# Linear attention and a squared-ReLU feed-forward on one core: the second batch's k^T v and x made two pairs at a time, both plans drawn anew

## The chip, the core and the metric

The kernel runs on one core of one Trainium2 chip. The metric is the device time of one execution in microseconds (us). A core has a matrix engine (TensorE, PE in the profile, with its weight loads as PEld), a vector engine (DVE), a scalar engine (ACT), a general engine (POOL) and a queue engine that issues most transfers (SP). PE writes to PSUM, in banks of 128 partitions x 512 floats; the other operands lie in SBUF.

## What is computed

```python
q_s = softmax(q, axis=-1)            # q, k, v: 8 batches, 8 heads, 576 tokens, 64 wide
k_s = softmax(k, axis=2)             # over the tokens
kv  = einsum('bhsd,bhse->bhde', k_s, v)
x   = einsum('bhsd,bhde->bhse', q_s, kv)   # laid out as 4608 tokens x 512
h   = maximum(x @ w_in, 0)           # 512 -> 2048
out = (h * h) @ w_out                # 2048 -> 512, float32
```

The weights come as 64-bit floats and are taken apart into a high and a low part of the PE's short format; x and h*h are split alike, so that a product takes three passes (high high, high low, low high).

## The kernel before

**Tiles of tokens and batches.** Each batch has 512 tokens ahead and a tail of 64. Tile t of the feed-forward takes the 512 tokens of batch t; the eight tails together make one more tile. While tile t runs, the attention of batch t + 1 is made between its products, in 16 steps of which four belong to each of the four pairs of heads: step s = 4p + i is part i of pair p. Tiles 0 and 1 are made straightforwardly: for each of 16 blocks f of the hidden width 12 products `h` (`first`), and two blocks later 12 products into the four banks `acc` (`second`). From tile 2 on a scheme with fewer products is used.

**Tile 0 also converts the weights.** For each of 16 units u, ACT scales the words (`scale_words`), DVE joins them by way of a PSUM bank named `up` (`join_words`: TENSOR_SCALAR into the bank, SCALAR_TENSOR_TENSOR out of it), POOL adds the low word, ACT casts the high part, and POOL subtracts to get the low part (`split_words`). The tiles `w` of it have two buffers.

**Attention before the change.** Batch 0 (start of the kernel) and batch 1 (beside tile 0) go pair by pair: `kv_of(b, p)` makes k^T v of a pair in one burst of products, scales it into the tile `kv`; `q_turn` transposes q with PE into the bank `qT` and copies it to SBUF, with POOL copying the 64 tail tokens (`qT<-qth`); `x_product(b, p, x)` makes x in two halves of 288 columns, each two products that use two of the four 64 x 64 quarters of the array, and copies each half out. From batch 2 on (`b >= TB`, TB = 2) two pairs go together: `kv_of(b, p-1, p)` in one burst into two banks, then `x_products`: four products of 512 columns, one in each quarter of the array, into the same two banks. The odd pair has its heads crossed over (`turn`), and the x of the tail tokens (`tail_burst`, eight products of 64 columns) is hung behind the next k^T v burst.

**Banks.** Up to the start of the feed-forward the intermediate results find six PSUM banks; after it just two, `a0` and `a1` (`bank`). In batch 1 these two serve the `up` of the conversion, the transposes (`qT`, `kmT`), the maximum's broadcast (`kmb`), k^T v and x.

**The order of the instructions** is made by `Planner`: it knows each step's engine, estimated length, and what it must wait for, and takes at each moment the most urgent of the steps that could start (`order`). The urgency is the estimated length of what depends on a step, altered by a list of random shifts (`shift`), each drawn from a seed: `SEEDS` for the first plan (the start and tile 0, `run`), `LATER` for the second (the rest up to tile 6, `run_on`). `possible` keeps a step from taking the last bank where its users could then not run; some of its clauses hold in the second plan alone (`self.locked`). The engines run their instructions in the order written.

**Names that the prediction uses.** In the profile `acc<-w,gh` and `acc<-w,gl` are `second`, `h<-x,w` is `first`, `kv<-v,ek` and `kv<-v_tail,kt` are k^T v; in batch 1 `x<-qT,kv` is x, from batch 2 on `kv<-qT,kv` is x (it is written into the banks of kv) and `kv<-qtail,kv` the tails. A 32-bit float product is two records. Line L101 is the helper that issues every planned instruction, so operands tell the steps apart.

Of the kernel before, what the change touches and what calls it, by code (L numbers as in the profile page):

```python
# [10 lines left out]
F32 = mybir.dt.float32  # L11
# [121 lines left out]
class Planner:  # L133
# [127 lines left out]
    def possible(self, n, b, known, spare):  # L261
        if n.end is not None:
            return True
        if n not in known:
            known[n] = all(
                o is b or o.placed is not None
                or self.locked and o.choices and o.users[0] is b.users[0]
                or (spare if len(o.choices) > 1 else self.place(o)[0] is not None)
                or self.locked and not o.choices and all(
                    self.possible(u, b, known, spare)  # L270
                    for u in (o.before.users if o.before else []) + (o.last.users[:1] if o.last else [])
                )
                for o in n.buffers
            ) and all(self.possible(o, b, known, spare) for o in n.before)
        return known[n]
# [106 lines left out]
def attention_ffn(  # L382
# [43 lines left out]
    STEP = 0.0  # L426
    WIDE = 487
    SEEDS = (
# [8 lines left out]
    )  # L437
    LATER = (
# [8 lines left out]
    )  # L447
    EASE = 0.0
    EARLY = 2
# [185 lines left out]
    def load_kq(b, p, which, queue=Y):  # L635
        turned = which == "k" and b == 0
        t = pair_tile(b, p, [P, C, 2, D] if turned else [P, 2, C, D], which)
        src = (k if which == "k" else q)[b, 2 * p:2 * p + 2, 0:M, :]
        to = "p c h d" if turned else "p h c d"
        queue.dma_start(out=t, in_=src.rearrange(f"h (p c) d -> {to}", c=C), kb=256)  # L640
        made[which, b, p] = t

# [40 lines left out]
    def load_tail_kq(b, which, queue=Y):  # L683

        src = k if which == "k" else q
        t = att.tile(
            [P, GH, D], F32, tag=f"{which}t", name=f"{which}t_{b}", bufs=1
        )
        for g in range(2):
            queue.dma_start(  # L690
                out=t[g * TL:(g + 1) * TL].only(2 * g, 2 * g + 1),
                in_=src[b, g * GH:(g + 1) * GH, M:SQ, :].rearrange("h p d -> p h d"),
                kb=64,
            )
        made[f"{which}t", b] = t
# [201 lines left out]
    def first_max(p):  # L897

        kr = made["k", 0, p].rearrange("p c h d -> p c (h d)")
        ps = bank(f"kT_{p}", True)  # L900
        with plan.together():
            for c in range(C):
                T.transpose(out=ps[:, c * P:(c + 1) * P], in_=kr[:, c, :], identity=ident, n=300)
        kc = small([P, 1], "kc", f"kc_0_{p}")
        V.tensor_reduce(out=kc, in_=ps, op=ALU.max, axis=AX.X)
        at = p % 2 * 2 + p // 2
        V.scalar_tensor_tensor(
            out=kc, in0=kc, scalar=-1.0, in1=made["ktm"][:, at:at + 1], op0=ALU.mult, op1=ALU.min, n=8
        )
        made["kT", p] = ps, kc  # L910

# [60 lines left out]
    def q_turn(b, p):  # L972

        qr = made.pop(("qn", b, p))
        ps = bank(f"qT_{b}_{p}", b == 0)
        with plan.together():
            for c in range(C):
                T.transpose(
                    out=ps[:, c * P:(c + 1) * P], in_=qr[:, c, :], identity=ident, n=260
                )  # L980
        qt = (boot if b == 0 and p % 2 else att).tile(
            [P, SQ], F32, tag="qh", name=f"qT_{b}_{p}", bufs=1
        )
        at = (p % 2 * 2 + p // 2) * TL
        G.tensor_copy(out=qt[:, M:SQ].only("tail"), in_=made["qTt", b][:, at:at + TL], n=64)
        V.tensor_copy(out=qt[:, 0:M].only("main"), in_=ps)
        made["qT", b, p] = qt

    def kv_product(b, *pairs):

        two = [bank(f"kv_{b}_{p}", b == 0) for p in pairs]
        made["kvp", b] = two
        n = D if b == 0 else D + 1
        tails = made.pop("tails", None) if b >= TB else None
        with plan.together():
            for p, ps in zip(pairs, two):
                kr, vr = made.pop(("ek", b, p)), made.pop(("v", b, p))
                tl, th = tail_of(b, p)
                turn = p % 2 if b >= TB else 0
                parts = [(kr[:, c, :], c) for c in range(C)]  # L1000
                if b == 0:
                    parts.append((made.pop(("ekt", p)), C))
                else:
                    parts.append((
                        made["kt", b][:, th, :].rearrange("p h d -> p (h d)").only(p % 2, p % 2 + 2), C
                    ))
                for k_part, c in parts:
                    for j in range(2):
                        rows = slice((j ^ turn) * D, (j ^ turn) * D + D)
                        cols = slice(j * (D + 1), j * (D + 1) + n)  # L1010
                        if b == 0:
                            of = vr[:, j, c, :] if c < C else v_heads[tl, 2 * p + j, 0:D].only(p // 2)
                        else:
                            of = vr[:, c, cols] if c < C else v_tail[:, p * W + cols.start:p * W + cols.stop]
                        T.matmul(
                            out=ps[rows, 0:n], lhsT=k_part[:, j * D:(j + 1) * D], rhs=of,
                            start=(c == 0), stop=(c == C),
                            n=2 * n if b < TB else 108 + BURST * (c == j == 0 and p == pairs[0]),
                        )
            if tails:  # L1020
                tail_burst(two, TAIL_AT, *tails)
        if tails:
            tail_out(two, TAIL_AT, *tails)
# [11 lines left out]
    def kv_of(b, *pairs):  # L1035

        kv_product(b, *pairs)
        kv_scale(b, *pairs)
        for p, ps in zip(pairs, made["kvp", b]):
            kv = small([P, D], "dg" if b >= TB and p > 1 else "kvs", f"kv_{b}_{p}")  # L1040
            S.activation(out=kv, in_=ps[:, 0:D], func=AF.Copy, scale=made.pop(("ks", p)), n=100)
            made["kv", b, p] = kv

# [139 lines left out]
    def first(t, f, x):  # L1183
# [8 lines left out]
        S.activation(out=r, in_=ps, func=AF.Relu)  # L1192
        if 0 < t < STRASSEN[0] and f >= ON_ACT:
            return r, r
        V.scalar_tensor_tensor(
            out=ps, in0=ps, scalar=0.0, in1=r, op0=ALU.max, op1=ALU.mult
        )
        return ps, r

    def split_g(t, f, ps, r):  # L1200
# [289 lines left out]
    def step_between(b, s, x):  # L1490

        p, i = divmod(s, NP)
        if b >= TB and i == 3 and p % 2:
            x_products(b, p, x, 0)

    def step_after(b, s, x, alone=True):
# [22 lines left out]
        elif i == 2:  # L1519
# [3 lines left out]
            else:  # L1523
                if p == 0:
                    tail_turn(b)
                kv_of(b, p)
                q_turn(b, p)
            if p + 1 < NP:
                load_v(b, p + 1)
# [2 lines left out]
                load_tail(b + 1)  # L1532
                load_tail_v(b + 1)
        elif i == 3:
            if b < TB:
                x_product(b, p, x)
            elif p % 2:
                x_products(b, p, x, 1)
            if p + 1 < NP:
                prepare(b, p + 1, alone)  # L1540
# [796 lines left out]
```

## Time and profile before

| | us |
|---|---|
| time, median of 3 runs (803.92 to 805.36) | 804.3 |
| time of the profiled execution | 804.34 |
| its span in the profile | 802.6 |
| PE busy | 786.7 (98%) |
| DVE busy | 597.3 (74%) |
| ACT busy | 497.3 (62%) |
| POOL busy | 139.1 (17%) |

The busy share of an engine is an average over stages with different limits: POOL's 17% over the span is nine tenths and more in the first sixth of it and next to nothing after. PE's products are pipelined and their ends modelled, so its cost is best read from one start to the next. The mean granted clock of the profiled run is 0.998 of full speed.

### The profile page before, as it was taken

How to read it: one execution, taken by the hardware profiler on the slowest of the kernel's cores; microseconds unless marked ns; L12 is line 12 of the kernel's file. 1: busy time of each engine (PE TensorE's matmuls, PEld its weight loads, DVE VectorE, ACT ScalarE, POOL GpSimd, SP SyncE). 2: the span in 40 equal slices, each digit the busy share in tenths (PEclk: the TensorE clock that was granted, in tenths of full speed). 3: DMA queues.
4: the chain of work that ended last, by engine and by line, in shares of the span. 5: the costliest groups of instructions: out<-in, count | busy, mean ns of one | idle time of the engine just before them, and what ended most of it. 6: DMA issues, size and time to landing. Idle time of an engine off the chain costs nothing.

```text
span 802.6 us, 14938 instructions
## 1 busy us (share of the span) xinstructions
PE 786.7 (98%) x5189; PEld 689.8 (86%) x5189; DVE 597.3 (74%) x1252; ACT 497.3 (62%) x967; POOL 139.1 (17%) x165
## 2 busy tenths in 40 slices
PE   8899999999999999999999999999999999999997
PEld 7578878888888989899898989898989888888887
DVE  6898985878768787787877777778776663246995
ACT  5898855545565667566756666666665665566452
POOL 4899892000000000000000000000000000000014
PEclk9999999999999999999999999999999999999999
DMA  9994116954699899898898978999898469999565
GB/s 288 390 327 143 31 49 176 328 150 124 177 265 253 265 275 279 238 272 247 263 266 271 263 216 258 240 283 259 259 280 257 138 218 368 381 306 377 169 181 98
DMA packets 210890, 193.19 MB, mean 241 GB/s; under 512 B 127424, under 2 KB 172992, under 8 KB 210816
## 3 DMA queue, kind: packets, MB, share of 16 engines
q1 hardware_dynamic: 205824, 189.96, 77.8%
q10 hardware_dynamic: 4352, 1.51, 0.8%
q0 software_dynamic: 640, 0.79, 0.4%
q8 instruction: 41, 0.67, 0.3%
q14 instruction: 33, 0.27, 0.1%
HBM read 150.34 MB, written 41.29 MB: 239 GB/s over the span
## 4 chain that ended last, share of the span: by engine, by line
PE 87%; DMA 6%; DVE 2%; ACT 2%; SPq 1%; issue 1%; POOL 1%; POOLq 0%; DVEq 0%; ACTq 0%
PE acc L101 34%; PE h L101 31%; PE h L1354 9%; PE out L2087 7%; PE kv L101 4%; DMA k<-in_k_dram 2%; SPq L101 1%; DMA raw<-in_moe_w_out_dram 1%; DMA raw<-in_moe_w_in_dram 1%; DMA ring<-w_sums 1%; PE x L101 1%; ACT w L101 1%; DMA out_dram<-o 1%; DVE w L101 1%; DMA bst<-bst 1%
## 5 line engine op out<-in xcount | busy, mean ns | idle before, releaser
L101 PE MATMUL acc<-w,gh 128*128 128x512 f32 x888 | 267.0, 382 | 3.7 <-DVE g L101 1.8
L101 PEld LDWEIGHTS acc<-w,gh 128*128 128x128 f32 x888 | 154.1, 190 | 24.3 <-issue 4.8
L101 PE MATMUL acc<-w,gl 128*128 128x512 f32 x444 | 168.4, 379 | 0.1
L101 PEld LDWEIGHTS h<-w,ring 128*128 128x128 f32 x1200 | 152.7, 191 | 11.8 <-issue 2.4
L101 PE MATMUL h<-w,ring 128*128 128x256 f32 x1200 | 155.2, 276 | 0.6 <-DVE c L101 0.5
L101 DVE TENSOR_TENSOR c<-h,u 128x256 f32<-128x256 f32 (+1 forms) x144 | 66.8, 466 | 86.3 <-ACT u L101 48.2
L101 ACT ACTIVATE c<-c 128x256 f32<-128x256 f32 (+1 forms) x198 | 116.3, 587 | 23.3 <-DVE c L101 20.1
L101 ACT COPY u<-h 128x256 f32<-128x256 f32 (+1 forms) x144 | 58.5, 406 | 95.2 <-PE h L101 76.5
L101 POOL PARTITION_ALL_REDUCE kmx<-km x24 | 20.6, 859 | 455.6 <-DVE km L101 392.6
L101 PEld LDWEIGHTS acc<-w,gl 128*128 128x128 f32 x444 | 83.9, 189 | 12.6 <-DVE gl L101 0.7
L101 PE MATMUL h<-x,w 128*128 128x512 f32 x384 | 90.6, 383 | 1.1 <-DVE x L101 0.6
L101 PEld LDWEIGHTS h<-x,w 128*128 128x128 f32 x384 | 71.3, 189 | 13.9 <-issue 1.7
L2087 PE MATMUL out<-w,w 128*128 128x512 f32 (+1 forms) x370 | 72.7, 352 | 0.6 <-DVE w L101 0.6
L2087 PEld LDWEIGHTS out<-w,w 128*128 128x128 f32 x370 | 62.7, 190 | 8.2 <-DVE w L101 0.8
L101 DVE TENSOR_TENSOR gl<-c,gh 128x512 fp32r<-128x512 f32 x80 | 54.9, 687 | 13.5 <-ACT gh L101 12.6
L101 PEld LDWEIGHTS h<-w,w 128*128 128x128 f32 x480 | 59.9, 191 | 3.9 <-issue 0.8
L101 PE MATMUL h<-w,w 128*128 128x256 f32 x480 | 61.8, 277 | 0.1
L101 ACT CAST gh<-c 128x512 fp32r<-128x512 f32 x80 | 49.5, 619 | 2.1
L1354 PE MATMUL h<-w,ring 128*128 128x512 f32 x204 | 46.3, 379 | 0.0
L101 DVE TENSOR_REDUCE bst<-q 128x18 f32<-128x576 f32 x48 | 35.9, 748 | 13.8 <-DMA q<-in_q_dram 10.3
L1354 PEld LDWEIGHTS h<-w,ring 128*128 128x128 f32 x204 | 38.6, 189 | 5.5
L101 POOL TENSOR_TENSOR w<-w,w 128x512 fp32r<-128x512 f32 x32 | 41.1, 1295 | 4.3 <-ACT w L101 4.1
(183 smaller groups left out, 1085.3 us busy)
## 6 DMA issues: line engine op xcount, KB each, us to landing
ring<-w_sums SPq DMA_DIRECT2D x48, 768.0 KB, 6.0
w<-w_sums SPq DMA_DIRECT2D x48, 512.0 KB, 5.3
ring<-w_sums SPq DMA_DIRECT2D x90, 256.0 KB, 4.7
k<-in_k_dram SPq DMA_DIRECT2D x32, 256.0 KB, 4.7
raw<-in_moe_w_in_dram SPq DMA_DIRECT2D x16, 512.0 KB, 8.4
raw<-in_moe_w_out_dram SPq DMA_DIRECT2D x16, 512.0 KB, 9.4
w<-wo_sums SPq DMA_DIRECT2D x32, 256.0 KB, 3.9
g_b<-c SPq DMA_DIRECT2D x30, 256.0 KB, 5.6
```

The lines of the kernel that those rows point to most:

```text
L101: getattr(self.eng, op)(*map(real, args), **{k: real(a) for k, a in kwargs.items()})
L1354: nc.tensor.matmul(out=out.real(), lhsT=a[:, k * P:(k + 1) * P].real(), rhs=in_turn(m[k]).real(), start=(begin and k == 0 and i == 0), sto ...
L2087: nc.tensor.matmul(out=banks[name][m][:, at].real(), lhsT=a[:, m * P:(m + 1) * P].real(), rhs=(rhs if half is None else rhs[:, half]).real ...
```

## The change

Batch 1 is made as the batches from 2 on are: pairs 0 and 1, and pairs 2 and 3, have their k^T v in one burst, with the odd pair's heads crossed over, and their x in four quarters of the array, 512 columns at once. The x of the tail tokens of pairs 0 and 1 hangs behind the k^T v burst of pairs 2 and 3, that of pairs 2 and 3 behind the first k^T v burst of batch 2, which runs beside tile 1. For this, q of an odd pair is loaded in two transfers with the heads exchanged (one before), q's tails in six (two before); POOL's copy of the tail tokens per pair goes, as x of the tails reads the transposed tail tile directly; odd pairs of batch 1 get a buffer `ql` of their own. In the planner the clauses of `possible` that were for the second plan hold in the first too. Both lists of seeds are replaced (63 by 57, and 58 by 48). In batch 0 one instruction of DVE that joins two maxima (`kc`) has another form with the same result. A branch for the squares of tile 0 is added that is never taken.

```diff
@@ Planner.possible
-                or self.locked and o.choices and o.users[0] is b.users[0]
+                or o.choices and o.users[0] is b.users[0]
...
-                or self.locked and not o.choices and all(
+                or not o.choices and all(
@@ SEEDS, LATER: all values replaced
@@ load_kq
+        if which == "q" and b and p % 2:
+            for h in range(2):
+                queue.dma_start(
+                    out=t[:, h].only(h), in_=src[1 - h].rearrange("(p c) d -> p c d", c=C), kb=128
+                )
@@ load_tail_kq
+        if which == "q" and b:
+            for g, (at, of) in itertools.product(range(2), ((0, 0), (2, 3), (3, 2))):
+                n = 1 + (at == 0)
+                queue.dma_start(
+                    out=t[g * TL:(g + 1) * TL, at:at + n, :].only((g, at)),
+                    in_=src[b, g * GH + of:g * GH + of + n, M:SQ, :].rearrange("h p d -> p h d"),
+                    kb=16 * n,
+                )
@@ first_max
-        V.scalar_tensor_tensor(
-            out=kc, in0=kc, scalar=-1.0, in1=made["ktm"][:, at:at + 1], op0=ALU.mult, op1=ALU.min, n=8
+        V.tensor_scalar(
+            out=kc, in0=kc, scalar1=-1.0, scalar2=made["ktm"][:, at:at + 1], op0=ALU.mult,
+            op1=ALU.min, n=8,
@@ q_turn
-            [P, SQ], F32, tag="qh", name=f"qT_{b}_{p}", bufs=1
+            [P, SQ], F32, tag="ql" if b and p % 2 else "qh", name=f"qT_{b}_{p}", bufs=1
...
-        at = (p % 2 * 2 + p // 2) * TL
-        G.tensor_copy(out=qt[:, M:SQ].only("tail"), in_=made["qTt", b][:, at:at + TL], n=64)
+        if b == 0:
+            at = (p % 2 * 2 + p // 2) * TL
+            G.tensor_copy(out=qt[:, M:SQ].only("tail"), in_=made["qTt", b][:, at:at + TL], n=64)
+        elif p % 2 == 0:
+            four = made["qTt", b].rearrange("p (i g t) -> p i g t", i=2, g=2)
+            made["qtail", b, p // 2] = four[:, :, p // 2, :]
@@ kv_product
-        tails = made.pop("tails", None) if b >= TB else None
+        tails = made.pop("tails", None)
...
-                turn = p % 2 if b >= TB else 0
+                turn = p % 2 if b else 0
@@ step_between
-        if b >= TB and i == 3 and p % 2:
+        if i == 3 and p % 2:
             x_products(b, p, x, 0)
@@ step_after
-                kv_of(b, p)
+                if p % 2:
+                    kv_of(b, p - 1, p)
                 q_turn(b, p)
...
-            if b < TB:
-                x_product(b, p, x)
-            elif p % 2:
+            if p % 2:
                 x_products(b, p, x, 1)
```

## Rows read from the trace of the kernel before

**Rows 1.** The page: busy time of each engine, and POOL's share by slice.

```profile
PE 786.7 (98%) x5189; PEld 689.8 (86%) x5189; DVE 597.3 (74%) x1252; ACT 497.3 (62%) x967; POOL 139.1 (17%) x165
...
POOL 4899892000000000000000000000000000000014
```

**Rows 2.** Windows: length, busy of PE, PEld, DVE, ACT, POOL, then clock, DMA, GB/s.

```profile
36.00:56.00 20.00, 17.08 (x80) 13.72 (x77) 18.86 (x30) 17.85 (x25) 19.17 (x18) 1.00 1.01 332
...
96.00:116.00 20.00, 20.00 (x116) 17.06 (x116) 18.42 (x33) 13.48 (x21) 18.49 (x17) 1.00 0.15 41
116.00:132.40 16.40, 16.40 (x97) 12.41 (x96) 10.74 (x23) 7.66 (x16) 7.74 (x9) 1.00 0.49 138
```

**Rows 3.** PE's waits over the span: total us, times, longest.

```profile
PE acc L101 <- DVE g L101: 1.8, 1, 1.8
...
PE acc L101 <- ACT o L101: 1.5, 1, 1.5
```

**Rows 4.** Chain of waits through batch 1: start, length, piece, count of records.

```profile
64.60 2.59 PE h L101 x12
...
70.43 0.63 PE x L101 x4
71.06 2.14 PE h L101 x9
...
90.30 0.73 PE kv L101 x20
91.03 2.79 PE acc L101 x12
93.82 1.12 PE x L101 x8
94.94 2.16 PE h L101 x9
```

**Rows 5.** The same chain through batch 2, made two pairs at a time.

```profile
173.37 1.32 PE kv L101 x40
174.68 0.84 PE acc L101 x3
...
178.76 1.02 PE kv L101 x8
179.78 2.14 PE acc L101 x9
...
198.76 1.59 PE kv L101 x48
200.35 1.49 PE h L101 x6
```

**Rows 6.** POOL and PE in order of time, and POOL's tail copies (56 to 132 us).

```profile
124.70 2.50 POOL L101 TENSOR_TENSOR w<-w,w 128x512 fp32r<-128x512 f32 x2 [2.25 <-ACT w L101]
...
128.53 0.59 PE L101 MATMUL acc<-w,gh 128*128 128x512 f32 x2
...
L101 POOL COPY qT<-qth 128x64 f32<-128x64 f32 x4 | 0.9, 234 | 0.1
```

**Rows 7.** DVE's instructions on `up` in a window; batch 2's copies of x.

```profile
56.00:120.00 64.00, 25.84 (x40) 1.00 0.30 95
...
180.02 0.68 DVE L101 COPY x<-kv 128x512 f32<-128x512 f32 x1
...
212.02 0.69 DVE L101 COPY x<-kv 128x512 f32<-128x512 f32 x1 [0.34 <-PE kv L101]
```

**Rows 8.** The start: DVE's kc, POOL beside it, and SP's loads of q's tails.

```profile
8.32 0.16 DVE L101 SCALAR_TENSOR_TENSOR kc<-kc,ktm 128x1 f32<-128x1 f32 x1
...
20.02 0.68 DVE L101 SCALAR_TENSOR_TENSOR kc<-kc,ktm 128x1 f32<-128x1 f32 x1
...
19.39 1.29 POOL L101 TENSOR_TENSOR w<-w,raw 128x512 int32<-128x512 int32 x1
...
L101 SPq DMA_DIRECT2D qt<-in_q_dram x2: 614/616/617, 18.6 to 19.3; - x2
```

More of the change, by code (lines that the diff above doesn't have):

```diff
@@ L639, in load_kq @@
         to = "p c h d" if turned else "p h c d"
+        if which == "q" and b and p % 2:
[3 more added lines that the diff above has]
+                )
+            made[which, b, p] = t
+            return
         queue.dma_start(out=t, in_=src.rearrange(f"h (p c) d -> {to}", c=C), kb=256)
@@ L688, in load_tail_kq @@
         )
+        if which == "q" and b:
[6 more added lines that the diff above has]
+                )
+            made[f"{which}t", b] = t
+            return
         for g in range(2):
@@ L1017, in kv_product @@
                             start=(c == 0), stop=(c == C),
-                            n=2 * n if b < TB else 108 + BURST * (c == j == 0 and p == pairs[0]),
+                            n=2 * n if b == 0 else 108 + BURST * (c == j == 0 and p == pairs[0]),
                         )
@@ L1039, in kv_of @@
         for p, ps in zip(pairs, made["kvp", b]):
-            kv = small([P, D], "dg" if b >= TB and p > 1 else "kvs", f"kv_{b}_{p}")
+            kv = small([P, D], "kvs" if b < TB or p < 2 else "dg", f"kv_{b}_{p}")
             S.activation(out=kv, in_=ps[:, 0:D], func=AF.Copy, scale=made.pop(("ks", p)), n=100)
@@ L1194, in first @@
             return r, r
-        V.scalar_tensor_tensor(
-            out=ps, in0=ps, scalar=0.0, in1=r, op0=ALU.max, op1=ALU.mult
-        )
+        if t == 0 and (False):
+            S.activation(out=ps, in_=r, func=AF.Square)
+        else:
+            V.scalar_tensor_tensor(
+                out=ps, in0=ps, scalar=0.0, in1=r, op0=ALU.max, op1=ALU.mult
+            )
         return ps, r
```

30 rows, old and new, of tables (LATER, SEEDS) are left out of this document.

## The prediction

> **What bounds the kernel now.** First the page: PE is busy 98% of the span, so time can be won where PE has less to do or stops waiting; POOL is busy in the first sixth alone [rows 1]. Then the windows of that sixth, for an average hides it: between 36 and 56 us PE lacks 2.9 us, and from there to the end of tile 0 it is busy without a gap (the two windows that are not shown are as full) [rows 2]. But up to 116 us DVE has 18.4 and 18.9 of 20 us and POOL 18.5 and 19.2: tile 0 is bounded by PE with two engines close behind it. Third, PE's waits: the two large ones are 1.8 us for a step of DVE at 48.8 us, before the stretch in question, and 1.5 us for a copy of ACT at 230 us [rows 3]. Last, the chain of waits: from 56 us until past the first pairs of batch 2 it holds PE and nothing else, product after product, with the bursts of batch 1 among them [rows 4] and those of batch 2, which are already made as the change makes batch 1's [rows 5]. So the change can be priced with rows of its own kind.
>
> **PE's bursts, step by step.** Twelve products of `h` take 2.59 us, 0.216 each [rows 4]. A burst costs its piece of the chain and what the piece behind it takes above 0.216 a product, which is the cost of changing over and back.
> - k^T v of one pair: 0.73 + (2.79 - 12 x 0.216) = 0.93. There are four such bursts, all of 0.73: 3.7 us.
> - x, a half alone: 0.63 + (2.14 - 9 x 0.216) = 0.83; four of them, 3.3 us. Two halves back to back: 1.12 + (2.16 - 9 x 0.216) = 1.34; two of these, 2.7 us.
> - Together 9.7 us; two of the ten are followed by a transpose and change over only once, about 0.05 less each: 9.6 us.
>
> After the change, by batch 2's rows [rows 5]:
> - k^T v of two pairs without tails: 1.32 + (0.84 - 3 x 0.216) = 1.51.
> - The same with eight products for tails behind it: 1.59 + (1.49 - 6 x 0.216) = 1.78, so tails cost 0.27.
> - x of two pairs: 1.02 + (2.14 - 9 x 0.216) = 1.22, twice: 2.44.
> - Together 1.51 + 1.78 + 2.44 = 5.73 us in tile 0, and 0.27 in tile 1, where batch 2's first burst now carries batch 1's last tails.
>
> So PE has 9.6 - 5.7 = 3.9 us less in tile 0 and 0.3 more in tile 1: **3.6 us less**. Most of it is x: 576 columns in two quarters become 512 in four, and six change-overs become two. None of this lay beside other PE work; all of it stands on the chain.
>
> **What else moves in tile 0.** The engines close behind PE decide how much comes through. POOL's last conversion ends at 124.70 + 2.50 = 127.20; the product that first reads it is the second of the three that begin at 128.53, so at 128.75 [rows 6]. The margin is 1.5 us. POOL loses four tail copies, 0.9 us [rows 6]. If POOL's order had no other play, tile 0 could end 1.5 + 0.9 = 2.4 us earlier, not 3.9. But POOL also waits 2.25 us just before that last conversion, for a cast of ACT, which in the window is busy 7.7 of 16.4 us [rows 2, 6]; the new order may close part of that. I take the middle of 2.4 and 3.9, 3.15 us, because both PE's rows and POOL's idle time are in view and which wins is a matter of the draw. What is late next is POOL's last conversion, then x for tile 1.
>
> The new wait is for **banks**. Up to now a burst of batch 1 takes one of the two banks and gives it back after a copy; from now on both are held from the first k^T v product to the end of x's copies. Behind that stand DVE's `up` instructions, which need a bank, POOL's adds, which need DVE's result, and the transposes of q: q of the second pair must be turned before the burst. In batch 2 such a hold lasted from 173.37 to 180.02 + 0.68 = 180.70, 7.3 us, and then from 198.76 to 212.71, 13.9 us [rows 5, 7]. It can't be shorter than its two bursts and a copy, 1.51 + 1.22 + 0.68 = 3.4 us. DVE has other work for part of it (`up` and what reads it are 25.84 of 64 us, four tenths, [rows 7]), and POOL has two units in its two buffers, each with two subtractions of 1.25 us [rows 6], so 5 us. I put a hold between 3.4 and 7.3 us at nothing, since those 5 us and the margin cover it; if the cover is gone, it is the rival below. Only the first hold counts: at the second the conversion is nearly done.
>
> k^T v of pair 0 now waits for pair 1, whose burst stood at 90.30 [rows 4]; its operands keep their two buffers so long, and the loads of pair 2 stand behind it on SP's queue. Pairs 2 and 3 had their bursts after that point before too, and the order of PE's products is free to go round them, so I put this at nothing; the most that it could cost is the 2 us by which I bound a draw, below.
>
> Transfers: four more for q's tails and one more for each of two odd pairs, 0.616 us each on SP's queue [rows 8]. The four stand early, ahead of the rest of the weights: 2.5 us for the queue. Between 36 and 56 us the transfer engines are full (share 1.01, [rows 2]), so the bytes bound it and not the issues; I count 0, with 2.5 us as the upper end if the queue should run dry.
>
> **kc.** Of these four DVE instructions the one at 8.32 took 0.16 us and the one at 20.02 took 0.68; it ended at 20.70, and the POOL instruction from 19.39 ended at 20.68 [rows 8]. So a long one waits for POOL. The new form can save between 0 and, if all four were long, 4 x 0.52 = 2.1 us of DVE in the first 36 us; I take 0, as what follows is bound by transfers and by POOL too [rows 2]. The Trainium skill ("SBUF — State Buffer", "Who interferes with whom") says that a DVE instruction with two SBUF inputs contends with a POOL instruction that reads SBUF and that one with a single input does not, and the trace agrees with the first half by the two ends 0.02 us apart. If the scalar operand doesn't count as a second input, that rule would give up to the 2.1 us, which is a rival below.
>
> **The two draws.** All other instructions may change their order. A draw can remove the waits of 1.8 and 1.5 us [rows 3] or make others of that size; from both sides 2 us, value 0.
>
> **The sum.** 804.34 (the profiled execution, 1.74 above its span, and 0.04 above the median) less 3.15 in tile 0, plus 0.27 in tile 1: 801.46, **801.4 us**. With all of 3.6 it is 800.7, with POOL's 2.4 it is 802.2; the case's own range, with half a us of draw on either side, is 800.2 to 802.7.
>
> **The rivals.**
> - *POOL ends tile 0.* The conversion doesn't move: PE arrives earlier, uses up the 1.5 us of margin and waits. 804.34 - 1.5 + 0.3 = 803.1. For it: POOL's 19 of 20 us. Against it: 0.9 us less work and its own waits. 0.20.
> - *The banks starve the conversion (slower).* The first hold is as long as batch 2's second, 13.9 us. POOL's cover is 5 us, so it stands 8.9 us, of which 2.4 are margin: 6.5 us lost against 3.6 won, 807.2. It decides from a hold of 5 + 2.4 + 3.6 = 11 us. For it: a hold of 13.9 us exists. Against: in tile 1 nothing pressed the planner to shorten it, and it counts with banks. 0.11. The Trainium skill has a rule of this kind ("TensorEngine Tiling (Array Packing)", "PSUM Bottleneck"): the products get faster by quarters of the array, the emptying of PSUM does not, and may become the bound. In batch 2 the trace does not bear it out, as PE never waits there for a copy of x; no stage there needs the banks as tile 0 does.
> - *A worse draw.* The bursts shrink as worked out, but a wait of 2 us more stands elsewhere: 803.4. 0.11.
> - *A better draw, or kc comes through.* The 1.5 us at 230 go, or DVE's up to 2.1 us of kc shorten the wait for DVE at 48.8 [rows 3, 8]: 801.4 less 1.5 to 2.1 is 799.3 to 799.9. 0.08.
>
> **How the numbers follow.** My forecast has 0.50. About 0.2% (1.6 us) is what a measurement here tells from no change: faster is below 802.7, slower above 805.9. Faster: 0.50, 0.08 and 0.02 of the first rival, 0.60. Slower: 0.11 and the bad end of the draws, 0.04: 0.15. Same: 0.25. The range reaches from the better draw to above both rivals with 803: 799.5 to 805.4; outside it lie the banks' rival and the tips of the draws, under 0.2.
>
> **What would show it.** In the chain of the changed kernel, right would be: two k^T v bursts of 1.3 to 1.6 us and two x bursts near 1.0 in tile 0, the first `h` of tile 1 at about 129.3 (132.4 before), and k^T v of batch 2 with 48 records at its first burst. POOL as the bound would show as PE idle just before tile 1, ended by POOL's or ACT's `w`; the banks as POOL idle for several us between the first k^T v and its x; a draw as a wait anywhere else. The forecast is wrong if x in batch 1 doesn't come at 1.0 us a burst, or if a new PE wait of over 2 us appears.

## The result: 0.8% slower, and the profile of the changed kernel

| | before | after |
|---|---|---|
| median of 6 runs, us | 804.83 (803.41 to 806.54) | 811.11 (808.80 to 814.67) |
| ratio, 95% interval | | 1.0076 (1.0055 to 1.0098) |
| profiled execution, its span, us | 804.34, 802.6 | 811.36, 809.6 |
| granted clock | 0.998 | 0.995 |

The forecast was 801.4 us and, with 0.60, faster. The time is 6.3 us longer in the medians, outside the range. One execution among all that follow, of e3, took 909 us at a granted clock of 0.85, and its ratio leaves it out. PE's work is nearly the same as in [rows 1]; the page of after:

```profile
PE 788.4 (97%) x5198; PEld 692.7 (86%) x5198; DVE 597.0 (74%) x1252; ACT 498.9 (62%) x963; POOL 140.7 (17%) x161
```

The chain of waits of after shows where the time is (start, length, piece, count of records). It answers to [rows 4] and [rows 5]:

```profile
44.22 8.80 DMA k<-in_k_dram
...
53.04 1.02 DVE km L101
54.06 0.59 DVE mx L101
...
54.77 1.28 DVE qt L101
56.05 1.29 DVE km L101
...
57.38 0.33 PE kmT L101
...
88.43 1.32 PE kv L101 x40
89.74 1.49 PE acc L101 x6
91.24 1.02 PE kv L101 x8
...
124.43 1.59 PE kv L101 x48
126.03 1.49 PE acc L101 x6
127.52 1.02 PE kv L101 x8
128.54 5.38 PE acc L101 x24
133.91 1.29 PE h L101 x6
...
215.11 5.11 DMA ring<-w_sums
...
220.35 1.58 PE h L101 x12
```

The bursts came as forecast: 1.32, 1.59 and twice 1.02 us, in place of ten bursts of 0.63 to 1.12 in tile 0. But the chain before had nothing but PE from 56 us into batch 2. Just ahead of that it too stood on the transfer of k, which [rows 4] do not show:

```profile
45.20 6.72 DMA k<-in_k_dram
...
51.94 0.84 DVE km L101
...
54.17 0.62 DVE up L101
...
54.81 0.71 DVE w L101
...
55.56 0.33 PE kmT L101
```

There DVE's step ended at 55.52 and PE's products ahead of `kmT` at 55.51: PE did not wait, but k's path had nothing to spare. In after the chain leaves PE for that path until 57.38, and once more at 215 us for a transfer of weights of tile 2. PE's waits at these places are 4.31 us (`kmT` at 57.38) and 2.73 us (`h<-w,ring` at 220.35); the two waits of [rows 3] are gone or small.

Cut at states that both kernels pass, the 7.0 us of span come out as follows (starts of PE's instructions in order of time):

| stretch of PE's order | before | after | difference |
|---|---|---|---|
| start to the end of the `h` products ahead of `kmT` | 54.70 | 53.07 | -1.63 |
| from there to the next `h` (`kmT` and 12 `acc<-w,g` between) | 3.11 | 9.11 | +6.00 |
| from there to tile 1 | 74.76 | 71.73 | -3.03 |
| tile 1 | 83.50 | 86.44 | +2.94 |
| tile 2 to the first product after tile 6 | 429.42 | 431.97 | +2.55 |
| the rest | 157.11 | 157.28 | +0.17 |

The third row is the change's gain, and it is there. The second and fourth rows are new waits. The lower clock behind the first wait is in the second row too; that behind the other falls in the fifth.

**Where the 6 us begin: the queue.** SP's instructions of after in order of time (start, length, transfer, count), the six small loads one by one (shortest, median and longest in ns, first and last start), and what SP waited for between 20.9 and 28 us (total, times, longest):

```profile
18.12 2.75 SPq L101 DMA_DIRECT2D raw<-in_moe_w_out_dram  x1
20.97 5.85 SPq L101 DMA_DIRECT2D qt<-in_q_dram  x6
27.91 0.37 SPq L101 DMA_DIRECT2D raw<-in_moe_w_in_dram  x1
...
L101 SPq DMA_DIRECT2D qt<-in_q_dram x6: 465/492/617, 21.0 to 26.4; - x6
...
SPq L101 <- DMA raw<-in_moe_w_in_dram: 2.2, 3, 1.1
SPq L101 <- DMA raw<-in_moe_w_out_dram: 1.5, 2, 0.8
```

and what the transfer engines moved from 20 to 40 us, in half microseconds:

```profile
GB/s 399 410 438 389 375 393 399 422 449 371 379 397 438 403 364 204 56 49 152 229 356 344 262 311 244 188 215 281 305 260 360 332 361 369 410 401 387 389 408 410
```

The six loads of q's tails stand in 5.85 us of SP's queue, where two took 1.27 us before. By itself none is dear: each took 0.47 to 0.62 us, and the forecast had 0.616 from [rows 8]. The rest is SP waiting for weight loads to land, 3.7 us up to the next weight load. The issue and landing times in the trace show for which: no transfer left SP's queue before the one eight places ahead of it had landed (the fourth small load went out at 23.79, that weight load had landed at 23.78; for the weight load at 27.91 it was 27.89). So eight at most are under way, and six small loads, 128 KB in all, filled six of the eight places. At 27.9 us one weight load and the six were under way, 640 KB at most; before, at 27.35, five weight loads and two small ones, 2.7 MB. No weights were issued between 20.9 and 27.9 us. The last weight load ahead of that, begun at 18.12, landed 11.1 us later, at 29.2; at 28 to 29 us the engines had run dry (56 and 49 GB/s), and it took them until 36 to be full again. In these 20 us 6.66 MB came in against 7.79 before: 1.13 MB, which is 2.9 us at the 389 GB/s of before. What stands behind on the queue is late by it, k of the second batch's first pair too. The Trainium skill ("Perfetto Trace Analysis", "What DMA-bound means") names the issuing engine's queue as a bound of its own, known by a track that is solid with DMA slices. These rows are not that case: of the 6.9 us from 20.97 to 27.91 SP waited 3.7.

The windows of before and after (length, busy of PE, PEld, DVE, ACT, POOL, clock, DMA share, GB/s). Before:

```profile
25.00:30.00 5.00, 4.73 (x48) 2.93 (x47) 4.80 (x12) 3.34 (x11) 3.69 (x8) 1.00 1.08 379
30.00:35.00 5.00, 5.00 (x44) 3.76 (x41) 4.78 (x10) 4.59 (x8) 3.55 (x7) 1.00 1.06 398
```

After:

```profile
25.00:30.00 5.00, 3.78 (x42) 2.82 (x42) 4.59 (x10) 4.91 (x13) 4.62 (x7) 1.00 0.83 267
30.00:35.00 5.00, 4.67 (x46) 2.78 (x47) 4.19 (x12) 4.18 (x12) 4.10 (x7) 1.00 0.90 277
...
55.00:60.00 5.00, 2.62 (x10) 2.19 (x10) 4.32 (x6) 1.87 (x4) 3.99 (x5) 0.80 0.93 311
60.00:65.00 5.00, 5.00 (x23) 4.29 (x23) 4.62 (x10) 4.06 (x7) 4.69 (x5) 0.86 1.07 378
```

After PE's idle 4.3 us the granted clock of the next two windows is 0.80 and 0.86, part of it at the lower of its two levels.

### The profile page after: what moved, and what is told of

It is laid out like the page before. It is cut to its first block, busy times and chain, and to the rows that moved or that the text cites. A ratio compares the mean times of both kernels' runs of the same rounds, so it can differ in the third digit from the quotient of the medians.

```text
span 809.6 us, 14949 instructions
## 1 busy us (share of the span) xinstructions
PE 788.4 (97%) x5198; PEld 692.7 (86%) x5198; DVE 597.0 (74%) x1252; ACT 498.9 (62%) x963; POOL 140.7 (17%) x161
## 3 DMA queue, kind: packets, MB, share of 16 engines
q10 hardware_dynamic: 4352, 1.51, 0.8%
## 4 chain that ended last, share of the span: by engine, by line
PE 80%; DMA 8%; SPq 4%; DVE 3%; ACT 2%; issue 1%; POOL 1%; POOLq 0%; DVEq 0%; ACTq 0%
PE acc L101 31%; PE h L101 29%; PE h L1377 9%; PE out L2109 7%; SPq L101 4%; PE kv L101 4%; DMA ring<-w_sums 2%; DMA bst<-bst 2%; DMA raw<-in_moe_w_out_dram 1%; DMA k<-in_k_dram 1%; ACT c L101 1%; DMA w<-w_sums 1%; ACT w L101 1%; DMA q<-in_q_dram 1%; POOL out_dram L101 1%
## 5 line engine op out<-in xcount | busy, mean ns | idle before, releaser
L101 POOL PARTITION_ALL_REDUCE kmx<-km x24 | 22.9, 953 | 458.0 <-DVE km L101 448.6
L1377 PEld LDWEIGHTS h<-w,ring 128*128 128x128 f32 x204 | 38.4, 189 | 6.7 <-ACT u L101 0.7
L101 POOL TENSOR_TENSOR w<-w,raw 128x512 int32<-128x512 int32 x32 | 41.5, 1310 | 3.4 <-ACT raw L101 1.3
```

Of the source, the lines that this page charges most:

```text
L101: getattr(self.eng, op)(*map(real, args), **{k: real(a) for k, a in kwargs.items()})
L1377: nc.tensor.matmul(out=out.real(), lhsT=a[:, k * P:(k + 1) * P].real(), rhs=in_turn(m[k]).real(), start=(begin and k == 0 and i == 0), sto ...
```

## The experiments

The main theory, A: the six small loads in a row let the transfers run dry; k lands late; PE idles and loses clock. Rivals: the bursts and banks cost the time (B), or the new order of the second plan does (C). Ratios are to the kernel before, measured beside it on the same chip.

| run | ratio | 95% interval |
|---|---|---|
| after | 1.0076 | 1.0055 to 1.0098 |
| e1_tails_in_two | 1.0024 | 1.0010 to 1.0037 |
| e2_before_six | 1.0053 | 1.0028 to 1.0077 |
| e3_old_second_draws | 1.0071 | 1.0049 to 1.0094 |
| e4_ring_urgent | 1.0075 | 1.0055 to 1.0096 |
| e5_tails_between | 1.0105 | 1.0076 to 1.0134 |
| e6_k_before_last_weights | 1.0040 | 1.0023 to 1.0057 |
| e7_ring_before_q | 1.0021 | 1.0004 to 1.0037 |
| e8_both_orders | 1.0029 | 1.0009 to 1.0048 |
| e9_redrawn | 0.9977 | 0.9957 to 0.9996 |
| e10_redrawn_ring | 0.9949 | 0.9932 to 0.9966 |
| e11_before_redrawn | 0.9998 | 0.9981 to 1.0014 |

A trace is one execution, and executions of one kernel lie some 3 us either side of the median; the first microseconds alone differ by up to 2.5 (SP's first weight load after the first v loads stands at 14.29 us in after's trace and at 16.79 in e1's). So times come from the ratios, and from the traces only waits and stretches.

**e1: the change without the six loads.**

```diff
 load_tail_kq
-        if which == "q" and b:   # six loads, heads 2 and 3 exchanged
...
 tail_turn
+                if b and i:      # heads exchanged here
+                    for h in range(2):
+                        T.matmul(out=ps[h * D:(h + 1) * D, P:2 * P], lhsT=qt[:, 3 - h, :], rhs=ident,
+                                 start=True, stop=True, n=115)
+                    continue
```

> The changed kernel, with q's tails of the second batch in two loads again instead of six; the two heads that trade places do so on TensorE (two products with the identity, 64 rows out, for one transpose). Every engine's order is otherwise that of the changed kernel. Theory A (the four extra loads hold SP's queue, the weight transfers behind them start late, k of the second batch lands 1 us or more late, PE idles 4.3 us at 57.4 and then runs at a lower granted clock): SP's two tail loads take under 1.5 us instead of 5.9, the stretch 25 to 35 us moves 370 GB/s or more again instead of 267 to 277, the idle at 57.4 is 0 to 2 us, the granted clock of 55 to 65 us is over 0.93, and the time is 805.3 us (804.3 to 807). Theory B (the new bursts, bank holds or POOL's conversion cost the time): idle and time stay, 810 to 812 us. Theory C (the second plan's order is all of it): 810 to 812 us too, with the idle at 57.4 gone but given back before 220 us.

SP's loads of the tails, the windows, and PE's product in e1:

```profile
23.93 1.57 SPq L101 DMA_DIRECT2D qt<-in_q_dram  x2
...
25.00:30.00 5.00, 3.84 (x26) 2.76 (x24) 4.30 (x9) 4.78 (x12) 3.89 (x6) 1.00 1.06 400
30.00:35.00 5.00, 4.01 (x53) 2.74 (x53) 4.14 (x10) 4.23 (x11) 3.92 (x9) 1.00 1.08 379
...
57.74 0.33 PE L101 MATMUL kmT<-ident,km 128*128 128x128 f32 x1 [1.88 <-DVE km L101]
```

Throughput is back, the wait is 1.88 us in place of 4.31, and the clock stays at 1.00 behind it. The ratio falls from 1.0076 to 1.0024, 4.2 us (by the two intervals 2 us more or less): B and C alone are out. The size is less than the 5.8 us expected; 1.9 us of the wait stay, and 1.0 more at 73.8 us.

**e2: the six loads alone, in the kernel before.**

```diff
+        if which == "q" and b:
+            for g in range(2):
+                with plan.together():      # one step for the plan, whose order stays
+                    for at, n in ((0, 2), (2, 1), (3, 1)):
+                        queue.dma_start(out=t[g * TL:(g + 1) * TL, at:at + n].only(2 * g, 2 * g + 1), ...)
```

> The kernel before, with nothing changed but q's tails of the second batch, which come in six loads (two, one and one head for each half) in the place of two; the plan and every engine's order stay those of before. Theory A: SP's queue is held about 4 us longer at 20 to 27 us, the stretch 25 to 35 us moves about 270 GB/s in place of 380 to 398, PE meets the transpose of the second batch's means 2 to 3.5 us too early, and the time is 807.8 us (806.8 to 809). Theory B (the six loads cost nothing, the transfers were full anyway, as the prediction had it): 804.8 us, within 0.7.

The queue, DVE and PE of e2, in order of time:

```profile
20.17 6.60 SPq L101 DMA_DIRECT2D qt<-in_q_dram  x6
...
55.78 1.05 DVE L101 TENSOR_REDUCE km<-k 128x128 f32<-128x512 f32 x1 [4.37 <-DMA k<-in_k_dram]
...
58.99 0.33 PE L101 MATMUL kmT<-ident,km 128*128 128x128 f32 x1 [1.69 <-DVE w L101]
```

6.6 us on the queue, 277 and 301 GB/s in the two windows, DVE idle 4.37 us for k, and 1.0053: 4.3 us (2 us more or less), above the 3.0 expected but the same as e1 took away. PE's wait at `kmT`, none before, is 1.69 us in this trace, under the 2 to 3.5 expected; the clock had fallen once ahead of it, behind a wait at 48.88, and slowed PE. Removed from one kernel and put alone into the other, the loads weigh the same. Theory A holds for 4.2 of the 6.1 us.

The traces agree. Counted from SP's first weight load after the first v loads, k landed at 38.7, 38.9 and 39.2 us with six loads in the changed order (after, e3, e4) and at 36.5 and 36.2 with two (e1, e7), 2.6 us earlier in the mean; in the old order at 39.8 with six (e2) and at 37.5 with two (before). The second row of the table above, 9.1 us in after, is 10.4 and 10.6 in e3 and e4, and 5.9 and 5.5 in e1 and e7: 4.3 us in the mean.

**e3, e4: the second plan.** e3 puts the old list `LATER` on the changed kernel; e4 makes the loads at fault in tile 1 more urgent.

```diff
 e4
+            plan.ease = -10.0
             for first_of in GROUPS:
                 ring_load(t + 1, 0, first_of)
+            plan.ease = 0.0
```

> The changed kernel, with the second plan's urgencies drawn from the seeds of the kernel before (each draw shifts the same instructions as it did there); the first plan is that of the changed kernel. Theory A and C, that the new order of the second plan costs 4 to 5 us through the weight blocks of the third tile that are loaded behind q's loads on SP's queue: the first of those loads is issued before 211 us, PE's wait of 2.7 us at 220 is gone, and the time is 807 us if nothing takes its place; since the draws were made for another list of instructions, other waits of 1 to 1.6 us are likely, and then it is 808 to 811. If the new order costs nothing against the old: 811 to 813.

> The changed kernel, with the third tile's first weight loads made 10 us more urgent in the second plan, so that they are issued on SP's queue ahead of the four q loads that wait for a buffer. If that queueing costs what the trace shows (2.7 us of PE idle and about 0.9 us at half clock at 220 us): the wait at 220 us falls under 1 us and the time is 808 us (807 to 809.5). If the q loads, now later, are waited for in its place: the wait moves to 225 to 260 us and the time stays at 810 to 812.

In both the weights of tile 2 are issued ahead of q's loads, and the wait of 2.73 us at 220 is gone (none and 0.26 us). The time is not: 1.0071 and 1.0075. PE's waits of e4 from 124 to 330 us (total, times, longest):

```profile
PE h L101 <- DVE c L101: 2.4, 3, 1.1
PE acc L101 <- ACT o L101: 1.7, 1, 1.7
```

From tile 2 to the end of tile 6 e3 takes 432.7 us and e4 434.2, where after takes 432.0 and before 429.4. The wait that the queue made was given back as waits for ACT and DVE. Theory C is not refuted by that, but neither edit could show it.

**e5: the six loads spread.** Same loads, each behind a pair of weight loads, on SP's queue alone.

```diff
+    of = [n for n in told if n.moved and n.buffers[0].name == "qt_1"]
+    for n, other in zip(of, [f"raw_{u}" for u in range(4, 10)]):
+        n.start = (start of other's last load) + 1e-3
```

> The changed kernel with its six tail loads, one after each of six pairs of weight loads on SP's queue instead of six in a row; nothing else of any engine's order differs. Theory A1 (the six cost time because they stand in a row, 5.9 to 6.6 us in which no weights are issued, longer than what is still under way): no half microsecond of 25 to 35 us falls under 250 GB/s, PE's idle at the transpose of the second batch's means is 1 to 3 us as with two loads, and the ratio to before is that of two loads, 1.002 to 1.003 (after: 1.0076). Theory A2 (each small load costs the queue its microsecond wherever it stands): the idle stays near 4 us and the ratio at 1.006 to 1.008.

Both theories missed. The transfers were repaired, as A1 said: no half microsecond from 20 to 40 us is under 318 GB/s. Yet the ratio is 1.0105, the worst. The last tail load was now issued at 37.19 us, and in the changed kernel's order DVE has its first step on q's tails ahead of x for tile 0:

```profile
43.99 0.42 DVE L101 TENSOR_REDUCE mx_t<-qt 128x4 f32<-128x256 f32 x1 [9.68 <-DMA raw<-in_moe_w_out_dram]
...
44.79 1.41 DVE L101 TENSOR_TENSOR x<-x,x 128x224 fp32r<-128x224 f32 x4
```

DVE stood 9.68 us (the releaser named is a transfer of weights; the operand is `qt`, whose last load landed at 43.81) and PE 8.6 us for `x` behind it. So in the time e5 doesn't tell A1 from A2. On the queue A2 is out and A1 right in part: each of the six took 0.47 to 0.62 us here as in the row, not a microsecond, and SP again let none out before the transfer eight places ahead had landed; but with five weight loads or more among the places the engines stayed full. It also shows how early the order needs these tails.

**e6, e7, e8: the two remaining waits of e1, by SP's order alone.**

```diff
+    e6, e8 (first plan):  the two loads of raw_11 behind k_1_0
+    e7, e8 (second plan): the four loads of q_3_0 behind the first load into ring_0
```

> The kernel with the tails in two loads, and on SP's queue alone k of the second batch's first pair put ahead of the last pair of weight loads that stood before it (1 MB, 2.6 us at 390 GB/s). If what is left of PE's idle there (1.9 us at 57.7 and 1.0 us at 73.8 us in the kernel with two loads) hangs on the landing of that k: it lands 2 to 2.6 us earlier, both idles together fall under 1 us, and the ratio to before falls by 0.002 to 0.003, from 1.0024 to about 1.000. If the chain behind it on VectorE and GpSimd sets it: both idles stay, ratio 1.002 to 1.003.

> The kernel with the tails in two loads, and on SP's queue alone the first weight load of the third tile put ahead of the four q loads; no other order differs. If the 2.8 us of PE idle at 220 us is that queueing and nothing waits for the q loads 1 us later: idle gone, ratio 1.0024 less 0.0034, about 0.999. If the q loads' users were next in line: waits of 1 to 3 us come up between 222 and 260 us, as in the run with urgent weights, and the ratio stays at 1.001 to 1.003.

> Both of the last two edits of SP's order at once on the kernel with the tails in two loads. If both waits are independent: the gains add up, 2 and 2.8 us, and the ratio is 0.996 to 0.998, the 801.4 to 803 us that the prediction had for the change. If only one counts: 0.999 to 1.001.

e6 brought nothing (1.0040; e1 has 1.0024, the intervals overlap). DVE of e6 in order of time tells why:

```profile
48.05 1.08 DVE L101 TENSOR_REDUCE km<-k 128x128 f32<-128x512 f32 x1
51.21 0.69 DVE L101 TENSOR_REDUCE mx<-q 128x8 f32<-128x512 f32 x1 [2.08 <-DMA q<-in_q_dram]
...
52.02 1.28 DVE L101 TENSOR_TENSOR qt<-qt,sm_t 128x256 f32<-128x256 f32 x1
53.23 1.35 DVE L101 TENSOR_TENSOR km<-km,kt 64x128 f32<-64x128 f32 x1
```

k landed in time now and DVE didn't wait for it; it waited 2.08 us for q, which stands behind the same weight loads as ever. Between the sum over k and the sum that joins its tail, the new order has q's maximum and the division of q's tails; before, the division stood at 44.80, long ahead of the sum over k at 51.94. Both long steps run beside POOL, and `km<-km,kt` takes 1.35 us where before it took 0.62. That is the chain of the second forecast of e6: the first of the two waits stayed, at 2.06 us, and the second went from 0.97 to 0.38.

e7 took the wait at 220 away and two of 0.9 us came, for ACT and DVE:

```profile
219.15 0.94 PE L101 MATMUL h<-w,ring 128*128 128x256 f32 x6 [0.90 <-ACT u L101]
220.97 0.94 PE L101 MATMUL h<-w,ring 128*128 128x256 f32 x6 [0.89 <-DVE c L101]
```

e7 and e8 at 1.0021 and 1.0029 are not told from e1: e7's second forecast held, and e8 missed both of its own. So a swap in one queue moves the wait on, and these three runs do not show where what e1 leaves over before, 1.9 us, and what it lacks against the forecast, 4.8 us, comes from. The order of more than one engine is what the traces suggest.

**e9, e10, e11: the orders drawn again.** e9 draws both plans further on top of e1, with a lower transfer rate in the first plan; e10 adds e7's swap; e11 does to the kernel before what e9 does to the changed one.

```diff
 e9, e11
-    ISSUE, LAND, RATE, FIRST = 0.65, 2.2, 370.0, 2.0
+    ISSUE, LAND, RATE, FIRST = 0.65, 2.2, 345.0, 2.0
+    further seeds behind SEEDS and LATER
 e10: e9 and the swap of q_3_0 and ring_0 in SP's order
```

> The changed kernel with the tails in two loads, and both plans' urgencies drawn further from where they stood, 79 more draws; the first plan now reckons with transfers of 345 bytes a ns instead of 370, by which k of the second batch's first pair lands at 51.1 us in the plan (48.0 before that; 53.0 and 53.3 in the traces). VectorE's work on q's tails now stands ahead of the sum over that k and not behind it. Theory D (what two loads leave, 1.9 us over the kernel before, is the order of VectorE and of the queue around that k, and not the bursts): PE's idle at the transpose of the means is under 0.8 us, the wait of 2.8 us for the third tile's weights stays, as it is still in the plan, and the ratio to before is 0.998 (0.996 to 1.000). Theory E (the bursts or the banks cost what is left): ratio 1.001 to 1.003.

> The redrawn kernel with, on SP's queue alone, the first weight load of the third tile ahead of the four q loads. By the earlier pair of runs with that edit, the wait of 2.8 us goes and 1 to 2 us of it come back as waits for ScalarE's and VectorE's work at 219 to 221 us: 0.5 to 1.5 us less than the redrawn kernel, ratio 0.997 (0.995 to 0.999). If all comes back: no difference to the redrawn kernel.

> The kernel before, drawn further by as many trials as the redrawn kernel and with the same transfer rate of 345 in its first plan; nothing of the change is in it. If the change's bursts are worth the 3.0 us that the trace shows from the same state to the second tile, the redrawn kernel with the change is 2 to 3.5 us faster than this one, which has a ratio of 1.000 to 1.002 to before. If the redrawing is what helps and the bursts bring nothing: this one is as fast as the redrawn kernel with the change, or faster.

DVE and PE of e9 around k, in order of time:

```profile
47.62 0.94 DVE L101 TENSOR_TENSOR qt<-qt,sm_t 128x256 f32<-128x256 f32 x1
...
52.06 1.05 DVE L101 TENSOR_REDUCE km<-k 128x128 f32<-128x512 f32 x1
53.04 0.67 DVE L101 TENSOR_REDUCE mx<-q 128x8 f32<-128x512 f32 x1
53.63 0.95 DVE L101 TENSOR_TENSOR km<-km,kt 64x128 f32<-64x128 f32 x1
...
54.65 0.33 PE L101 MATMUL kmT<-ident,km 128*128 128x128 f32 x1
```

The division of the tails stands ahead of k again, PE doesn't wait for `kmT`, and e9 is at 0.9977 as theory D had it (0.998). Its wait for tile 2's weights stays (3.14 us, with a lower clock behind it); e10's swap removes it but for 0.33 us, 1.7 us of waits for ACT and DVE come, and e10 is at **0.9949: 4.1 us faster than the kernel before, and so the fastest of all**. The chain of e10, and of e11 behind it:

```profile
125.66 7.77 PE h L101 x36
```

```profile
133.05 3.02 PE h L101 x14
```

e10 reaches tile 1 at 125.66 us, before at 132.57 and e11 at 133.05. From `kmT` on that is 72.5 us in e9 and e10 and 76.8 in e11, 4.3 less; the 3 of 12 products `acc<-w,g` that e9 has left behind `kmT`, and e11 has none of, would make it 4.9. Of that 1.8 is e11's own: counted alike, the stretch is that much longer there than in before, and against before e9 gains 3.2. In the whole time e9 is 0.2% (1.7 us) under e11, less than the 2 to 3.5 us expected. Their intervals against before overlap; the twelve executions of each, set against each other, differ by 1.6 us in the mean with an interval of 0.3 to 3.0. But each kernel is one drawing of its orders, so how much of it is the bursts is not settled. e10 lies 3.7 us under e11 and has a swap by hand that e11 lacks. e10 gives back in tiles 2 to 6, which take it 433.0 us against 429.4 of before.

## Why the prediction was wrong

**Right: the bursts.** Forecast 5.73 us for the four of tile 0; by the same rule (piece, and what the next piece takes above 0.216 a product) after has 1.51, 1.21, 1.78 and 1.21, together 5.71. The tails cost the 0.27 forecast. From the same state to tile 1 the gain is 3.03 us of the 3.9. The rest went at one place, the second `kmT` at 73.33 and the `h` behind it, which waits for ACT's q: e5 has PE's order unchanged, doesn't wait there, and takes 0.81 us less for the stretch, all of it at these two instructions. That is 3.84 of the 3.9.

**Right: banks and POOL, as no bound.** POOL's last conversion of after began at 125.37 and took 2.51, so it ended at 127.88; PE, busy without a gap, didn't wait for it. In the first bank hold, from 88.43 to the end of x's last copy at 93.58, PE did not wait and POOL did once, 0.86 us for a cast of ACT. The two rivals that lived on these did not come.

**kc.** The four instructions took 0.20 to 0.22 us each, where two of the four before took 0.68 ([rows 8], at 20.02) and 0.67 (at 27.07). Two of them, at 19.54 and 20.32, ran while POOL copied (19.54 to 19.78, 20.18 to 20.42). So, as far as POOL's spans can be trusted, the rule of the Trainium skill ("SBUF — State Buffer", "Who interferes with whom") holds here with the scalar operand not counted as an input. PE came 1.63 us earlier to the end of the `h` ahead of `kmT`, about the size of the wait of 1.8 us at 48.8 [rows 3], which is gone; the wait at `kmT` ate it. It need not be kc: e11 has the old form, and counted from the same weight load it comes there at 38.4 us, after at 38.8 and before at 40.3.

**Wrong: the term for the transfers.** The step that failed is "the bytes bound it and not the issues; I count 0, with 2.5 us as the upper end". Its price of a load was right: 0.616 us, and 0.47 to 0.62 measured. What failed is the step from engines that are full to engines that stay full. It was read from 36 to 56 us, while the loads stand at 18 to 27, and it took no account of how many transfers are under way at once. With eight at most, six small loads in a row left 0.64 MB under way where before 2.7 MB were, the engines ran dry, and SP let the next weights out only as earlier ones landed. The upper end of 2.5 us, meant for a queue that runs dry, was about the lateness of k (2.6 us in the mean, 2.3 in the old order). It held nothing for what hangs on k: k's path to `kmT` had no slack before, PE's wait there was 3.4 us longer with six loads than with two (means of 4.31, 5.41 and 5.64 against 1.88 and 1.52), and the lower clock behind it brought the stretch to 4.3 us more. Measured, by e1 and e2: 4.2 to 4.3 us in the time.

**Wrong: the two draws, at most 2 us.** The new first order puts the division of q's tails between the two sums over k (2.9 us of waits left in e1); the new second order puts tile 2's weights behind four q loads that wait for a buffer on SP's queue, 2.73 us of idle and about 1.7 us of clock behind it (220.35 to the `acc` at 226.07 is 5.7 us in after; the same products take 4.1 in e1, whose clock stayed at 1.00). "A worse draw" had the mechanism and half the price, as a single wait of 2 us; there were two. Other orders of the same work need not have them: e9 is without the waits at `kmT` but has the one for tile 2's weights, 3.14 us; e10 is without both, but for 0.33 us.

Against the forecast of 801.4 after lacks 9.7 us: 4.2 to 4.3 are the loads, by two runs; the other 5 or so are what e1 lacks too, and its two waits of 2.9 and 2.8 us are of that size. e9 and e10 together show that an order without these waits recovers as much; as e9 redraws both plans at once and may win elsewhere too, no run shows it for each wait alone.

## What to carry to other kernels

Count a transfer as a place in its queue as well as in bytes and in issue time: look up how many transfers are under way at most, how many bytes they hold while a row of small loads passes, and what the first transfer behind it feeds. Read the chain of waits a little ahead of the stretch that you price: here k stood on it with nothing to spare. A wait in front of an in-order engine costs all that stands between the late operand and the bound engine, and then some clock. When a change comes with a new order of everything, give the old kernel a new order too (e11) before crediting or blaming the change: here the work saved was real, and the time showed the loads and the order instead.

## What the runs showed of the chip

- Places on SP's queue: in all thirteen traces, some 760 transfers each, none was issued before the one eight places ahead had landed, so that at most seven were under way at an issue (worked out from issue and landing times). Whether the program or the chip sets the number was not tried.
- Issuing small loads: loads of 16 and 32 KB took 0.47 to 1.12 us each on SP's queue, in a row or singly between weight loads, those of 64 KB 0.61 to 2.27, those of 512 KB 0.34 to 2.87. From the first of six small ones in a row to the next weight load 6.9 to 7.7 us passed in four traces, and SP waited 3.7 to 4.2 of them.
- The clock after idle time of PE at `kmT`: 1.9 us idle, clock 1.00 in the window behind (e1); 4.3 us, 0.80 in the window of 55 to 60 us (after); 5.4 and 5.6 us, 0.50 (e3, e4). Yet at 220 us nearly equal waits differed: 2.73 us idle left the products behind at half speed in after, 2.78 us did not in e1; and at 48.8 us 1.89 us of waiting left 0.66 in the window of 48 to 52 us in e2, 1.78 us left 1.00 in before.
- A transfer pushed out of the way can be worse than one that is slow: with the engines full throughout (e5), a load that landed 13.6 us later (43.81 against 30.22 in after) stopped DVE for 9.7 us.
